# A gated recurrence with routed experts: the last group's loads split into 384 and 64 tokens, and the last block of zeros issued earlier

## Chip, cores and metric

The kernel runs on one core of a Trainium2 chip. The metric is the device time of one execution in microseconds. The kernel before was timed three times; its profile comes from one more execution, taken by the hardware profiler.

## What is computed

First a gated recurrence over 5056 tokens of 4 batches with 256 channels, then a router that gives each of the 20224 tokens to one of 8 experts, of which each keeps the 80 tokens with the largest gate weight. All other rows of the output are zero.

```python
sig = 1.0 / (1.0 + np.exp(-f_logit))
f = lower_bound + (1.0 - lower_bound) * sig          # x, f_logit: (4, 5056, 256)
for t in range(S):
    h = f[:, t] * h + (1.0 - f[:, t]) * x[:, t]
    y[:, t] = h
x = y.reshape(20224, 256)
logits = x @ w_gate                                  # 8 experts
expert_idx = np.argmax(logits, axis=1)
gate_w = softmax(logits)[np.arange(N), expert_idx]
out = np.zeros((N, D))
for e in range(8):
    tok_idx = where(expert_idx == e), the 80 with the largest gate_w
    h = np.maximum(x[tok_idx] @ w1[e], 0.0)          # w1: 256 x 1024
    out[tok_idx] = gate_w[tok_idx, None] * (h @ w2[e])
```

## The kernel before

**Front.** The tokens are taken in 10 groups of 512 (`n_grp`), the last of which (`LAST`, group 9) has 448 in each batch (`TAIL`). A group and a batch make a unit: 40 units, numbered n = 4 x group + batch. A unit loads a tile `f_t` and a tile `x_t` of 128 partitions x 4 tokens x 256 channels, 512 KB each (`load`, L236 and L238). Units of the last group load 512 tokens as well: they start 64 tokens sooner (`tiles`, L156), and `turn_u` and `decay` leave the first 64 out. Then ScalarE takes the sigmoid (`gate`), GpSimd multiplies (`enter`), PE turns both tiles so that channels lie on partitions (`turn_s` into `sp` banks, `turn_u` into `up` banks), ScalarE writes the decay factors into `h_all` (`decay`, L269), DVE runs the recurrence along the tokens (`scan`, L277), and PE makes the router's logits (`logits`). The order is written out by hand: the loop over n from L407 runs `load` four units ahead, `gate` and `enter` two, the turns and `decay` one. Eight buffers (`ring`) hold the loaded tiles, so the load of unit n + 4 waits until PE has turned unit n.

**Ranking.** When the last unit's scan is done, DVE, PE and ScalarE find the 80 kept tokens of each expert; this is one long chain of small steps, mainly on DVE.

**Experts.** For each expert, tokens are copied out of `h_all` one at a time (`gather`), PE multiplies with `w1` (`hidden`) and `w2` (`result`), DVE scales (`finish`, tile `y`), and GpSimd writes 80 rows of the output with an indirect transfer (`scatter`, L783). The weights come as 32 halves of 512 KB (`half`), numbered in the order (1,0), (1,1), (2,0), (1,2), ... of matrix and expert, each matrix in two halves, through seven of the eight buffers: the eighth holds zeros by then. The very last half is loaded in two pieces.

**Zeros.** The output (20.7 MB) is zeroed by transfers that SP issues between the others: `clear` writes zeros from on-chip memory, `copied` (L138) copies the part of the output that is already zero. Some run in the front, many during the ranking, and the last ones between the weights, where the table `BETWEEN` (L529) says behind which half's issue a block stands; the last block has 256 KB. All scatters wait for all blocks of zeros.

All transfers but the scatters are issued by SP, in the order of the program. Each holds one of eight semaphores in turn, and waits until the one that had it before has landed, so SP never has more than eight transfers on their way.

Of the kernel before, what the change touches and what calls it, by code (L numbers as in the profile page):

```python
# [17 lines left out]
P = 128  # L18
# [8 lines left out]
def kernel(  # L27
# [114 lines left out]
    def clear(source):  # L142
# [10 lines left out]
        written[0] += rows * n  # L153

    def tiles(ap, b, g):
        return ap[b, ds(min(first(g), S - G), G)].rearrange("(p r) d -> p r d", r=R)  # L156

# [5 lines left out]
    with tc.tile_pool(name="gsm", bufs=1) as gsm:  # L163
# [69 lines left out]
        def load(n):  # L233
            g, b = divmod(n, B)
            fs[n] = slot(2 * n % NSLOT, "f_t").rearrange("p (r d) -> p r d", r=R)
            nc.sync.dma_start(out=fs[n], in_=tiles(f_logit, b, g))  # L236
            xs[n] = slot((2 * n + 1) % NSLOT, "x_t").rearrange("p (r d) -> p r d", r=R)
            nc.sync.dma_start(out=xs[n], in_=tiles(x, b, g))  # L238

        def gate(n):  # L240
# [7 lines left out]
        def turn_s(n):  # L248
            for o in range(DC):
                ps = pss.tile([P, G], F32, name="sp", tag="sp")  # L250
                for r in range(R):
                    nc.tensor.transpose(ps[:, ds(r * P, P)], sts[n][:, r, ds(o * P, P)], ident)  # L252
                sps[n, o] = ps
            del sts[n]

        def turn_u(n):
            for o in range(DC):
                ps = psu.tile([P, G], F32, name="up", tag="up")
                for r in range(R):
                    nc.tensor.transpose(ps[:, r::R], uts[n][:, r, ds(o * P, P)], ident)  # L260
                ups[n, o] = ps[:, G - size(n // B):]
            del uts[n]
# [3 lines left out]

        def decay(n):
            for o in range(DC):
                nc.scalar.activation(columns(n, o).rearrange("p (k r) -> p k r", r=R),  # L269
                                     sps.pop((n, o)).rearrange("p (r k) -> p k r", r=R)[  # L270
                                         :, P - run(n // B):],
                                     ACT.Identity, scale=nomlb[:, ds(o, 1)], bias=1.0)

        def scan(n):
            for o in range(DC):
                h = columns(n, o)
                nc.vector.tensor_tensor_scan(  # L277
                    h, h, ups.pop((n, o)),
                    h_all[:, o, ds(spot(n - B) + G - 1, 1)] if n >= B else 0.0,
                    ALU.mult, ALU.add)  # L280

        def logits(n):
# [22 lines left out]
        pairs_of.update({g: (g, g + 1) for g in range(LAST - 1, n_grp)})  # L305

        def by_token(g):
            k = run(g)
            ls = lss.pop(g)
            g0 = next(a for a, z in pairs_of.values() if a <= g < z)  # L310
            if g == g0:
                lts[g0] = plt.tile([P, 2, R, P], F32, name="lt", tag="lt")
            for j in range(R):
                nc.tensor.transpose(lts[g0][:k, g - g0, j], ls[:, j::R], ident)  # L314
# [88 lines left out]
        with tc.tile_pool(name="plg", bufs=1, space=PSUM) as plg, \  # L403
             tc.tile_pool(name="plt", bufs=1, space=PSUM) as plt:
            with tc.tile_pool(name="pss", bufs=2, space=PSUM) as pss, \
                 tc.tile_pool(name="psu", bufs=3, space=PSUM) as psu:
                for n in range(-AHEAD, n_unit):  # L407
# [526 lines left out]
```

## Time and profile before

| | us |
|---|---|
| median of three runs | 213.54 (213.47 to 214.17) |
| the profiled execution | 212.61 |
| its span, first to last instruction | 210.8 |
| PE busy | 178.6 (85%) |
| DVE busy | 156.0 (74%) |
| GpSimd busy | 143.2 (68%) |
| ScalarE busy | 133.4 (63%) |
| moved by DMA | 80.60 MB, mean 382 GB/s |

The span is shorter than the execution by what lies before the first and after the last instruction. The busy shares are means over three stages with different limits: the front (to about 126 us), the ranking (to about 152) and the experts. In the rows below PE is TensorE, DVE VectorE, ACT ScalarE, POOL GpSimd, and SPq the queue of SyncE, which issues transfers. "Releaser" is what ended a wait.

### The profile page before, as it was taken

The page shows a single profiled execution, that of the slowest core. Times are in us where ns is not written, and L with a number is a line of the kernel's source. Part 1 is how long each engine was busy: PE and PEld are TensorE (multiplying, and loading weights), DVE is VectorE, ACT ScalarE, POOL GpSimd, SP SyncE. Part 2 cuts the span into 40 slices and gives each one's busy share as a digit, 9 for nine tenths or more (in the row PEclk, how much of TensorE's full clock was granted, in tenths as well). Part 3 has the DMA queues.
Part 4 walks back from the last instruction along what each step waited for, and adds up shares of the span by engine and source line. Part 5 has one row for each costly group of instructions (what it writes and reads, how often), then busy time and mean ns, then how long its engine had stood idle before and what let it go on. Part 6 is the DMA issues. An engine that isn't in the chain of part 4 may idle for free.

```text
span 210.8 us, 6578 instructions
## 1 busy us (share of the span) xinstructions
PE 178.6 (85%) x2091; PEld 140.2 (66%) x2091; DVE 156.0 (74%) x399; ACT 133.4 (63%) x420; POOL 143.2 (68%) x287
## 2 busy tenths in 40 slices
PE   0499989997999999989999886689999697989870
PEld 0498868785878778777878763355586475767540
DVE  5159969999998999899798999975678756461010
ACT  4279789797787778777979872615666555360000
POOL 4848779799797889769897982416666565620372
PEclk9999999999999999999999999797999999999998
DMA  5999999999999999999999999999999999999621
GB/s 214 419 364 398 411 419 448 386 444 394 410 409 414 384 423 375 399 450 386 433 375 408 428 393 371 419 414 432 424 403 404 424 404 420 413 408 410 237 74 51
DMA packets 21362, 80.60 MB, mean 382 GB/s; under 512 B 2580, under 2 KB 2710, under 8 KB 20888
## 3 DMA queue, kind: packets, MB, share of 16 engines
q1 hardware_dynamic: 20936, 79.45, 94.1%
q0 software_dynamic: 384, 0.66, 1.1%
q8 instruction: 18, 0.29, 0.5%
q14 instruction: 24, 0.20, 0.2%
HBM read 72.62 MB, written 21.36 MB: 446 GB/s over the span
## 4 chain that ended last, share of the span: by engine, by line
DMA 34%; PE 33%; ACT 11%; DVE 8%; issue 5%; POOL 4%; ACTq 1%; POOLq 0%; SPq 0%; DVEq 0%
DMA w_sb<-in_moe_w_dram 19%; PE sp L252 11%; PE up L260 9%; DMA x_t<-in_x_dram 8%; PE lg L290 6%; DMA f_t<-in_f_logit_dram 6%; ACT h_all L269 5%; PE lt L314 2%; ACT xe L735 2%; POOL x_t L246 2%; DVE h_all L277 2%; ACT ls L299 2%; PE y_ps L770 2%; POOL out_dram L783 2%; PE h_ps L755 1%
## 5 line engine op out<-in xcount | busy, mean ns | idle before, releaser
L246 POOL TENSOR_TENSOR x_t<-f_t,x_t 128x1024 f32<-128x1024 f32 x40 | 94.8, 2373 | 21.1 <-DMA x_t<-in_x_dram 12.5
L277 DVE TENSOR_TENSOR_SCAN h_all<-h_all,up 128x512 f32<-128x512 f32 (+1 forms) x80 | 95.8, 1245 | 10.4 <-PE up L260 6.5
L269 ACT ACTIVATE h_all<-sp,nomlb 128x512 f32<-128x512 f32 (+1 forms) x80 | 50.3, 678 | 13.6 <-PE sp L252 12.8
L242 ACT ACTIVATE f_t<-f_t 128x1024 f32<-128x1024 f32 x40 | 42.4, 1059 | 11.6 <-DMA f_t<-in_f_logit_dram 9.8
L260 PE MATMUL up<-ident,x_t 128*128 128x128 f32 x320 | 43.8, 279 | 3.1 <-DVE h_all L277 1.8
L252 PE MATMUL sp<-ident,f_t 128*128 128x128 f32 x320 | 45.4, 287 | 0.0
L252 PEld LDWEIGHTS sp<-ident,f_t 128*128 128x128 f32 x320 | 35.9, 145 | 7.7 <-issue 7.3
L260 PEld LDWEIGHTS up<-ident,x_t 128*128 128x128 f32 x320 | 37.0, 144 | 5.0 <-DVE h_all L277 2.9
L735 ACT COPY xe<-h_all 128x2 f32 x256 | 25.4, 191 | 14.6 <-issue 14.1
L735 POOL COPY xe<-h_all 128x2 f32 x192 | 24.4, 187 | 14.6 <-issue 8.3
L770 PE MATMUL y_ps<-w_sb,hid 128*80 128x256 f32 x128 | 29.5, 382 | 4.6 <-DMA w_sb<-in_moe_w_dram 4.6
L735 DVE COPY xe<-h_all 128x2 f32 x192 | 22.6, 176 | 12.2 <-issue 11.0
L770 PEld LDWEIGHTS y_ps<-w_sb,hid 128*80 128x80 f32 x128 | 18.4, 150 | 13.5 <-issue 3.4
L290 PE MATMUL lg<-h_all,wg 128*32 128x128 f32 (+1 forms) x640 | 26.5, 282 | 0.8 <-ACT ls L299 0.6
L755 PEld LDWEIGHTS h_ps<-xe,w_sb 128*64 128x64 f32 x512 | 18.3, 138 | 5.7 <-issue 3.0
L755 PE MATMUL h_ps<-xe,w_sb 128*64 128x80 f32 x512 | 19.5, 234 | 1.0 <-DMA w_sb<-in_moe_w_dram 0.6
L290 PEld LDWEIGHTS lg<-h_all,wg 128*32 128x32 f32 x640 | 15.4, 108 | 7.2 <-issue 4.9
L783 POOL DMA_INDIRECT out_dram<-y,goal x8 | 7.5, 939 | 11.1 <-DMA w_sb<-in_moe_w_dram 9.0
L161 PE MATMUL warm<-h_all,ident 128*128 128x512 f32 x18 | 11.9, 807 | 0.0
L778 DVE TENSOR_SCALAR y<-y_ps,gates 80x256 f32<-80x256 f32 x8 | 3.8, 477 | 10.9 <-PE y_ps L770 10.5
L762 ACT ACTIVATE hid<-h_ps 128x320 f32<-128x320 f32 x8 | 3.5, 435 | 11.3 <-PE h_ps L755 5.8
L314 PE MATMUL lt<-ident,ls 128*128 128x128 f32 (+1 forms) x40 | 7.3, 306 | 3.7 <-ACT ls L299 3.7
(128 smaller groups left out, 98.8 us busy)
## 6 DMA issues: line engine op xcount, KB each, us to landing
f_t<-in_f_logit_dram SPq DMA_DIRECT2D x40, 512.0 KB, 6.4
x_t<-in_x_dram SPq DMA_DIRECT2D x40, 512.0 KB, 6.9
w_sb<-in_moe_w_dram SPq DMA_DIRECT2D x31, 512.0 KB, 9.9
out_dram<-out_dram SPq DMA_DIRECT2D x26, 512.0 KB, 9.8
out_dram<-zbuf SPq DMA_DIRECT2D x12, 512.0 KB, 10.4
out_dram<-h_all SPq DMA_DIRECT2D x1, 512.0 KB, 8.2
w_sb<-in_moe_w_dram SPq DMA_DIRECT2D x2, 256.0 KB, 8.8
out_dram<-out_dram SPq DMA_DIRECT2D x1, 256.0 KB, 9.4
```

Of the source, the lines that this page charges most:

```text
L161: nc.tensor.matmul(warm, ident, h_all[:, 0, :4 * P], start=True, stop=True)
L242: nc.scalar.activation(s_t, s_t, ACT.Sigmoid, scale=-1.0)
L246: nc.gpsimd.tensor_tensor(u_t, sts[n], u_t, ALU.mult)
L252: nc.tensor.transpose(ps[:, ds(r * P, P)], sts[n][:, r, ds(o * P, P)], ident)
L260: nc.tensor.transpose(ps[:, r::R], uts[n][:, r, ds(o * P, P)], ident)
L269: nc.scalar.activation(columns(n, o).rearrange("p (k r) -> p k r", r=R), sps.pop((n, o)).rearrange("p (r k) -> p k r", r=R)[:, P - run(n / ...
L277: nc.vector.tensor_tensor_scan(h, h, ups.pop((n, o)), h_all[:, o, ds(spot(n - B) + G - 1, 1)] if n >= B else 0.0, ALU.mult, ALU.add)
L290: nc.tensor.matmul(lgs[g][ds(q * LC, LC), b, :k].rearrange("p (m i) -> p m i", i=2), wg[:, o], pairs[:, :, q], start=o == 0, stop=o == DC ...
L735: copy(X[e][:, :, ds(k + j, 1)], h_all[:, :, ds(v, 1)])
L755: nc.tensor.matmul(ps[i][ds(s * H, H), c], wo[o][:, at:at + J * (H - 1) + 1:J], xt[:, o], start=o == 0 and c == 0, stop=o == DC - 1, skip_ ...
L770: marks[e, c] = nc.tensor.matmul(y, hid[:, c], halves[c // CH][:, c % CH], start=c == 0, stop=c == FC - 1, skip_group_check=True)
L783: sent.append(nc.gpsimd.indirect_dma_start(out=out, out_offset=bass.IndirectOffsetOnAxis(ap=goal[:, ds(e, 1)], axis=0), in_=rows.pop(e), i ...
```

## The change

The four units of the last group load their first 384 tokens only (three per partition). The other 64 tokens of each batch, in both tensors, come in eight transfers of 64 KB (64 partitions x 256 channels), which go into a part of `h_all` that is not in use yet. Two batches stand below each other, and two such pairs beside each other, so that all of them make one tile of 128 x 2 x 256 for each tensor. They are loaded with units 24 to 31, and get one sigmoid, one product, two times four turns and two decay steps of their own before unit 36 is scanned. The turned products stay in the second half of the `lt` bank, and each scan of the last four units is done in two instructions, 384 and 64 columns. In `BETWEEN` the last entry is 27 for 28.

```diff
     def tiles(ap, b, g):
-        return ap[b, ds(min(first(g), S - G), G)].rearrange("(p r) d -> p r d", r=R)
+        return ap[b, ds(first(g), rows(g) * P)].rearrange("(p r) d -> p r d", r=rows(g))
...
+        rest_f, rest_x = (h_all[:, :, ds(N - i * TAIL, D)] for i in (1, 2))
+
+        def load_rest(i):
+            of, to = ((f_logit, rest_f), (x, rest_x))[i // B]
+            j, c = divmod(i % B, B // DC)
+            nc.sync.dma_start(out=to[ds(c * REST, REST), j], in_=of[i % B, ds(S - REST, REST)])
+
+        def gate_rest():
+            nc.scalar.activation(rest_f, rest_f, ACT.Sigmoid, scale=-1.0)
+
+        def enter_rest():
+            nc.gpsimd.tensor_tensor(rest_x, rest_f, rest_x, ALU.mult)
...
+        def turn_rest(ps, of):
+            for o in range(DC):
+                for j in range(DC):
+                    nc.tensor.transpose(rest_of(ps, o)[:, ds(j * P, P)], of[:, j, ds(o * P, P)],
+                                        ident)
+            return ps
+
+        def decay_rest(sp):
+            for o in range(DC):
+                nc.scalar.activation(
+                    h_all[:, o, ds(LAST * GROUP, B * TAIL)].rearrange(
+                        "p (b t) -> p b t", t=TAIL)[:, :, TAIL - REST:],
+                    rest_of(sp, o).rearrange("p (b t) -> p b t", t=REST),
+                    ACT.Identity, scale=nomlb[:, ds(o, 1)], bias=1.0)
...
                 nc.vector.tensor_tensor_scan(
-                    h, h, ups.pop((n, o)),
+                    h[:, :m], h[:, :m], ups.pop((n, o)),
                     h_all[:, o, ds(spot(n - B) + G - 1, 1)] if n >= B else 0.0,
                     ALU.mult, ALU.add)
+                if g == LAST:
+                    nc.vector.tensor_tensor_scan(
+                        h[:, m:], h[:, m:], rest_of(rest_u, o)[:, ds(b * REST, REST)],
+                        h[:, ds(m - 1, 1)], ALU.mult, ALU.add)
...
+                    if 0 <= m - (TURN - 3 * B) < 2 * B:
+                        load_rest(m - (TURN - 3 * B))
+                    if n == TURN - 4:
+                        gate_rest()
+                    if n == TURN - 3:
+                        enter_rest()
+                    if n == TURN - 2:
+                        decay_rest(turn_rest(pss.tile([P, G], F32, name="sp", tag="sp"), rest_f))
+                    if n == TURN:
+
+                        bank = token_tile(LAST - 1)[:, 1].rearrange("p r k -> p (r k)")
+                        rest_u = turn_rest(bank, rest_x)
                     unit(gate, n + 2)
...
-    BETWEEN = (7, 8, 8, 14, 15, 20, 21, 25, 28)
+    BETWEEN = (7, 8, 8, 14, 15, 20, 21, 25, 27)
```

On SP, in the front (`f_t` and `x_t` are the units' tiles, `out_dram` the zeros), units 24 to 27 stand so before:

```order
L236 DMA f_t<-in_f_logit_dram 128x1024
L238 DMA x_t<-in_x_dram 128x1024
L236 DMA f_t<-in_f_logit_dram 128x1024
L238 DMA x_t<-in_x_dram 128x1024
L236 DMA f_t<-in_f_logit_dram 128x1024
L238 DMA x_t<-in_x_dram 128x1024
L236 DMA f_t<-in_f_logit_dram 128x1024
L238 DMA x_t<-in_x_dram 128x1024
L138 DMA out_dram<-out_dram 16x8192
```

and so the first three of them in the change, where the transfers into `h_all` are the 64 tokens:

```order
L244 DMA f_t<-in_f_logit_dram 128x1024
L246 DMA x_t<-in_x_dram 128x1024
L254 DMA h_all<-in_f_logit_dram 64x256
L244 DMA f_t<-in_f_logit_dram 128x1024
L246 DMA x_t<-in_x_dram 128x1024
L254 DMA h_all<-in_f_logit_dram 64x256
L244 DMA f_t<-in_f_logit_dram 128x1024
L246 DMA x_t<-in_x_dram 128x1024
L254 DMA h_all<-in_f_logit_dram 64x256
```

Behind each of eight units' loads one small transfer has come in; units 28 to 31 have those of `x`.

On SP, near the end of the experts, before (`w_sb` are weight halves, 128x1024 of `w1` and 128x2x512 of `w2`; in brackets what each waits for, DMAHW0 to DMAHW7 being the eight semaphores):

```order
L138 DMA out_dram<-out_dram 16x8192 [waits DMAHW2_49]
L517 DMA w_sb<-in_moe_w_dram 128x1024 [waits DMAHW3_49,PE_49]
L517 DMA w_sb<-in_moe_w_dram 128x1024 [waits DMAHW4_49,PE_49]
L523 DMA w_sb<-in_moe_w_dram 128x2x512 [waits DMAHW5_49,PE_49]
L138 DMA out_dram<-out_dram 16x4096 [waits DMAHW6_49]
L523 DMA w_sb<-in_moe_w_dram 128x2x512 [waits DMAHW7_49,PE_49]
```

and in the change:

```order
L141 DMA out_dram<-out_dram 16x8192 [waits DMAHW2_49]
L581 DMA w_sb<-in_moe_w_dram 128x1024 [waits DMAHW3_49,PE_49]
L581 DMA w_sb<-in_moe_w_dram 128x1024 [waits DMAHW4_49,PE_49]
L141 DMA out_dram<-out_dram 16x4096 [waits DMAHW5_49]
L587 DMA w_sb<-in_moe_w_dram 128x2x512 [waits DMAHW6_49,PE_49]
L587 DMA w_sb<-in_moe_w_dram 128x2x512 [waits DMAHW7_49,PE_49]
```

The last block of zeros (16x4096) and the weight half ahead of it have changed places, and with them their semaphores; the next half keeps its own.

On DVE, at the scans of units 36 and 37, before (`up` holds the turned products):

```order
L277 SCALAR_TENSOR_TENSOR h_all<-h_all,up 128x512 x2
L334 SCALAR_TENSOR_TENSOR eq<-cand,revexp 128x256
L277 SCALAR_TENSOR_TENSOR h_all<-h_all,up 128x448 x4
L343 TENSOR_REDUCE pick<-eq 128x32
L277 SCALAR_TENSOR_TENSOR h_all<-h_all,up 128x448 x2
```

and in the change:

```order
L386 SCALAR_TENSOR_TENSOR eq<-cand,revexp 128x256
L320 SCALAR_TENSOR_TENSOR h_all<-h_all,up 128x384
L325 SCALAR_TENSOR_TENSOR h_all<-h_all,lt 128x64
L320 SCALAR_TENSOR_TENSOR h_all<-h_all,up 128x384
L325 SCALAR_TENSOR_TENSOR h_all<-h_all,lt 128x64
L320 SCALAR_TENSOR_TENSOR h_all<-h_all,up 128x384
L325 SCALAR_TENSOR_TENSOR h_all<-h_all,lt 128x64
L320 SCALAR_TENSOR_TENSOR h_all<-h_all,up 128x384
L325 SCALAR_TENSOR_TENSOR h_all<-h_all,lt 128x64
L395 TENSOR_REDUCE pick<-eq 128x32
```

Each scan has become two, of which the second reads the `lt` bank and starts from the first one's last column.

## Rows read from the trace of the kernel before

**Rows 1.** DMA busy tenths in 40 slices of the span, from the page.

```profile
DMA  5999999999999999999999999999999999999621
```

**Rows 2.** Stretches: length; busy PE, PEld, DVE, ACT, POOL; PE clock, DMA share, GB/s.

```profile
30.00:110.00 80.00, 75.03 (x905) 62.06 (x905) 74.05 (x68) 66.17 (x91) 67.59 (x31) 1.00 1.02 409
110.00:150.00 40.00, 34.10 (x394) 24.05 (x396) 34.58 (x112) 23.71 (x86) 23.45 (x60) 0.91 1.02 410
150.00:198.00 48.00, 43.13 (x570) 31.94 (x566) 26.80 (x185) 24.27 (x220) 23.66 (x169) 1.00 1.01 406
198.00:211.00 13.00, 5.38 (x24) 3.52 (x24) 0.96 (x2) 0.00 (x0) 7.23 (x8) 0.94 0.23 71
```

**Rows 3.** The chain that ended last, shares of the span by line, from the page.

```profile
DMA w_sb<-in_moe_w_dram 19%; PE sp L252 11%; PE up L260 9%; DMA x_t<-in_x_dram 8%; PE lg L290 6%; DMA f_t<-in_f_logit_dram 6%; ACT h_all L269 5%; PE lt L314 2%; ACT xe L735 2%; POOL x_t L246 2%; DVE h_all L277 2%; ACT ls L299 2%; PE y_ps L770 2%; POOL out_dram L783 2%; PE h_ps L755 1%
```

**Rows 4.** Timeline of the tail: start, duration, engine, line, instruction, idle time before.

```profile
196.06 1.93 PE L770 MATMUL y_ps<-w_sb,hid 128*80 128x256 f32 x8
...
197.72 1.13 POOL L783 DMA_INDIRECT out_dram<-y,goal  x1 [8.96 <-DMA w_sb<-in_moe_w_dram]
...
198.75 5.38 PE L770 MATMUL y_ps<-w_sb,hid 128*80 128x256 f32 x24 [0.76 <-DMA w_sb<-in_moe_w_dram]
...
204.17 0.48 DVE L778 TENSOR_SCALAR y<-y_ps,gates 80x256 f32<-80x256 f32 x1 [2.97 <-PE y_ps L770]
...
206.45 0.91 POOL L783 DMA_INDIRECT out_dram<-y,goal  x1 [0.30 <-issue]
```

**Rows 5.** Transfers issued from 186 to 190 us: KB, median us to landing.

```profile
w_sb<-in_moe_w_dram SPq DMA_DIRECT2D x3, 512.0 KB, 9.9
out_dram<-out_dram SPq DMA_DIRECT2D x1, 256.0 KB, 9.4
```

**Rows 6.** Timeline of SP's queue near the end of the experts.

```profile
183.46 1.95 SPq L517 DMA_DIRECT2D w_sb<-in_moe_w_dram  x2
186.80 0.38 SPq L523 DMA_DIRECT2D w_sb<-in_moe_w_dram  x1
187.26 0.52 SPq L138 DMA_DIRECT2D out_dram<-out_dram  x1
188.74 3.86 SPq L523 DMA_DIRECT2D w_sb<-in_moe_w_dram  x4
```

**Rows 7.** DMA queues from 196 to 211 us: packets, MB, share of 16 engines.

```profile
q0 software_dynamic: 384, 0.66, 14.9%
```

**Rows 8.** DMA from 30 to 110 us, then from 3 to 8 us.

```profile
DMA packets 8173, 32.71 MB, mean 409 GB/s; under 512 B 996, under 2 KB 996, under 8 KB 8050
...
DMA packets 559, 2.00 MB, mean 401 GB/s; under 512 B 68, under 2 KB 70, under 8 KB 559
...
h_all<-in_moe_w_gate_dram SPq DMA_DIRECT2D x1, 8.0 KB
h_all<-in_lower_bound_dram SPq DMA_DIRECT2D x1, 1.0 KB
```

**Rows 9.** SP's queue around the first expert, and transfers issued from 146 to 147 us.

```profile
146.53 0.52 SPq L138 DMA_DIRECT2D out_dram<-out_dram  x1
149.41 0.35 SPq L517 DMA_DIRECT2D w_sb<-in_moe_w_dram  x1
...
150.73 0.38 SPq L523 DMA_DIRECT2D w_sb<-in_moe_w_dram  x1
...
out_dram<-out_dram SPq DMA_DIRECT2D x1, 512.0 KB, 10.9
```

**Rows 10.** Groups by shape from 100 to 130 us: count, busy us, mean ns.

```profile
L246 POOL TENSOR_TENSOR x_t<-f_t,x_t 128x1024 f32<-128x1024 f32 x8 | 19.1, 2381 | 3.0 <-DMA x_t<-in_x_dram 1.6 <-PE sp L252 1.0
L277 DVE TENSOR_TENSOR_SCAN h_all<-h_all,up 128x512 f32<-128x512 f32 x11 | 13.5, 1266 | 2.0 <-PE up L260 1.9
...
L277 DVE TENSOR_TENSOR_SCAN h_all<-h_all,up 128x448 f32<-128x448 f32 x8 | 8.6, 1124 | 0.0
```

**Rows 11.** Issues of the whole span: KB each, median us to landing, from the page.

```profile
f_t<-in_f_logit_dram SPq DMA_DIRECT2D x40, 512.0 KB, 6.4
```

More of the change, by code (lines that the diff above doesn't have):

```diff
@@ L69 @@
     assert TAIL % C == 0 and (GROUP & (GROUP - 1)) == 0
+    REST = TAIL % P
+    assert REST * B == DC * P and TAIL > P
     SEG = N // C
@@ L153, in clear, with rows @@
         written[0] += rows * n
+    def rows(g):
+        return size(g) // P
     def tiles(ap, b, g):
-        return ap[b, ds(min(first(g), S - G), G)].rearrange("(p r) d -> p r d", r=R)
+        return ap[b, ds(first(g), rows(g) * P)].rearrange("(p r) d -> p r d", r=rows(g))
     def busy(pool, m, tag):
@@ L234, in load, with rest_of @@
             g, b = divmod(n, B)
-            fs[n] = slot(2 * n % NSLOT, "f_t").rearrange("p (r d) -> p r d", r=R)
+            k = rows(g)
+            fs[n] = slot(2 * n % NSLOT, "f_t").rearrange("p (r d) -> p r d", r=R)[:, :k]
             nc.sync.dma_start(out=fs[n], in_=tiles(f_logit, b, g))
-            xs[n] = slot((2 * n + 1) % NSLOT, "x_t").rearrange("p (r d) -> p r d", r=R)
+            xs[n] = slot((2 * n + 1) % NSLOT, "x_t").rearrange("p (r d) -> p r d", r=R)[:, :k]
             nc.sync.dma_start(out=xs[n], in_=tiles(x, b, g))
+        rest_f, rest_x = (h_all[:, :, ds(N - i * TAIL, D)] for i in (1, 2))
[7 more added lines that the diff above has]
+            nc.gpsimd.tensor_tensor(rest_x, rest_f, rest_x, ALU.mult)
+        def rest_of(ap, o):
+            return ap[:, ds(o * B * REST, B * REST)]
+        def turn_rest(ps, of):
[11 more added lines that the diff above has]
+                    ACT.Identity, scale=nomlb[:, ds(o, 1)], bias=1.0)
         def gate(n):
@@ L250, in turn_s @@
                 ps = pss.tile([P, G], F32, name="sp", tag="sp")
-                for r in range(R):
+                for r in range(rows(n // B)):
                     nc.tensor.transpose(ps[:, ds(r * P, P)], sts[n][:, r, ds(o * P, P)], ident)
@@ L258, in turn_u @@
                 ps = psu.tile([P, G], F32, name="up", tag="up")
-                for r in range(R):
-                    nc.tensor.transpose(ps[:, r::R], uts[n][:, r, ds(o * P, P)], ident)
-                ups[n, o] = ps[:, G - size(n // B):]
+                k = rows(n // B)
+                for r in range(k):
+                    nc.tensor.transpose(ps[:, r:k * P:k], uts[n][:, r, ds(o * P, P)], ident)
+                ups[n, o] = ps[:, :k * P]
             del uts[n]
@@ L267, in decay @@
         def decay(n):
+            r = rows(n // B)
             for o in range(DC):
-                nc.scalar.activation(columns(n, o).rearrange("p (k r) -> p k r", r=R),
-                                     sps.pop((n, o)).rearrange("p (r k) -> p k r", r=R)[
-                                         :, P - run(n // B):],
+                nc.scalar.activation(columns(n, o)[:, :r * P].rearrange("p (k r) -> p k r", r=r),
+                                     sps.pop((n, o))[:, :r * P].rearrange("p (r k) -> p k r", r=r),
                                      ACT.Identity, scale=nomlb[:, ds(o, 1)], bias=1.0)
         def scan(n):
+            g, b = divmod(n, B)
+            m = rows(g) * P
             for o in range(DC):
@@ L305, with token_tile @@
         pairs_of.update({g: (g, g + 1) for g in range(LAST - 1, n_grp)})
+        def token_tile(g0):
+            if g0 not in lts:
+                lts[g0] = plt.tile([P, 2, R, P], F32, name="lt", tag="lt")
+            return lts[g0]
         def by_token(g):
@@ L311, in by_token @@
             if g == g0:
-                lts[g0] = plt.tile([P, 2, R, P], F32, name="lt", tag="lt")
+                token_tile(g0)
             for j in range(R):
```

## The prediction

> **What bounds the kernel now.** I read the line of DMA busy shares first: 9 in every slice from the second to the 37th [rows 1]. The table by stretch says the same with numbers: share 1.02, 1.02 and 1.01 at 409, 410 and 406 GB/s from 30 to 198 us, then 0.23 [rows 2]. No engine is as full: in the first stretch PE has 75.0 of 80 us, DVE 74.1, and in the expert stretch no one but PE is above 27 of 48. The chain of waits agrees: its largest line is the weight transfers [rows 3]. So up to 198 us the time is bytes over a rate, and after it there is a tail of 12.6 us in which hardly anything is moved.
>
> The tail has two strands [rows 4]. One is weights: the last transfer that PE waits for lands at 198.62 (issued at 188.74, 9.88 us later), PE does 24 multiplications from 198.75, and the last scaling of `y` stands at 204.17 + 0.48 = 204.65. The other is the scatters. All eight stand behind the last zero block; the first starts on GpSimd at 197.72 after 8.96 us of idling, they follow each other, and the eighth starts at 206.45, 1.80 after its `y` was ready. So the scatters end last, and their start is set by the zeros. (The row names a weight transfer as the releaser, and the zero block had landed at 187.26 + 9.4 = 196.66 [rows 5]; the first scatter's wait in the program is for the transfers that wrote zeros. A rival below takes the label at its word.)
>
> **The change part by part.** All is counted on the profiled execution: 212.61 us, of which 210.8 are the span and 1.8 lie around it. The median of the runs is 213.54, 0.93 more; I take a gain over from the one to the other unchanged.
>
> *The last zero block.* SP keeps eight transfers in flight: each waits for the one eight before it. That is why the block was issued at 187.26 and the weight half ahead of it at 186.80 [rows 6]. In the change these two swap their turns. The queues are served in order, so the block's bytes stand 512 KB sooner: 524,288 B / 406 GB/s = 1.29 us. Bounds: if only the issue counted, 187.26 - 186.80 = 0.46. If it could go right behind the half before it (the row at 183.46 ends at 185.41), 1.85; but the last `y` at 204.65 plus the 0.30 of idling that stands before a scatter caps the gain at 206.45 - 204.95 = 1.50. I take 1.29, nearest to a queue in order. The weight half that steps back lands 0.63 later (256 KB); PE took it up at 196.06, spent 1.93 on its eight multiplications and then waited 0.76 for the next half anyway, whose place does not move. That wait covers it; without it, it would cost 0.63 on the strand of `y`, which has 1.80 to give.
>
> *The bytes removed.* Units 36 to 39 load 384 tokens for 512, two tensors each: 8 x 128 rows lose 1 KB, 1,048,576 B / 409 GB/s = 2.56 us.
>
> *The bytes added.* Eight transfers of 64 rows of 1 KB: 524,288 B, by bytes 1.28 us. No load of such rows stands in the trace. The nearest rows from above are the scatters: 640 rows of 1 KB take 14.9% of 16 engines x 15 us = 35.8 us of engine time, 56 ns a row [rows 7], so 512 x 56 / 16 = 1.79 us. For a price per transfer there is the start of the program: 3 to 8 us holds the two smallest transfers of all, 8 KB and 1 KB, and still has 401 GB/s against the 409 of a stretch without any [rows 8]; 8/409 of 5 us is 0.10, 0.05 for each, which makes 1.28 + 8 x 0.05 = 1.68. The net saving is 2.56 - 1.28 = 1.28 at best, 0.77 by the scatters, 0.88 by the start. I take 0.9. The other end, far off, is a small transfer as dear as a 512 KB one, 1.28 each: 10.25 - 2.56 = 7.7 lost.
>
> A row can speak against this only for the placement: each of these transfers fills 64 partitions, and every large one of before fills 128. The Trainium skill (SBUF — State Buffer, "Door 1: The DMA port swizzle") says that partitions 0 to 63 reach only half of the DMA ports of the memory. By that rule the added bytes would take 2.56 us and the net saving would be 0; no run here shows it. It is the first rival.
>
> *Where the saving goes.* The loads are in the front; it reaches the end only if the queues never run dry between. The place to look is where SP waits for PE: the copy issued at 146.53 is the last before the first expert's weights free a buffer at 149.41 [rows 9]. That copy lands 10.9 later, at 157.4, so some 8 us of work were queued, and with 0.9 less it is 7 us. From 149.41 on SP issues again (three in 1.32 us), faster than they drain. So 0.9 arrives at every later landing, the last one at 198.62 included, and both strands of the tail move by it.
>
> *The engines in the front.* Cost in the sum: none, because of those 7 us. What they do all the same: DVE has 1266 ns for 512 columns and 1124 for 448 [rows 10], 2.2 ns a column and 138 fixed; so 384 + 64 columns cost 983 + 279 = 1262 for 1124, eight times, +1.1 us, on the stretch that leads to the ranking. GpSimd's product costs 2381 ns on 1024 elements; ¾ of that four times saves 2.4, and the product of the 64-token part adds half of one, 1.2, some units sooner. PE loses 16 transposes and gains 8. ScalarE gains three instructions, sigmoid and decay of the rest, and has shorter ones in the last four units. SP gains eight issues of about 0.33; it idles there. The rest waits for its loads nowhere, since they are issued 8 or more units ahead of their use. Even if all of it came late, DVE's 1.1 and one GpSimd product of 1.2, the ranking would slip by 2.3, and there are 7.
>
> *What is queued behind new waits.* On PE the four transposes of the rest need a free `sp` bank and those into the `lt` bank need the DVE step that read it; behind them stand the unit's own transposes, which free the load buffers. A stall of 1 to 2 us there takes from the 6.4 us that a load is on its way [rows 11] and leaves the queues full.
>
> **Sum:** 1.29 + 0.9 = 2.2 us. Span 208.6, execution 210.4, median 213.5 - 2.2 = **211.3**. The likeliest case's own range joins 0.46 to 1.50 with 0.77 to 1.28, so gains of 1.2 to 2.8: 210.7 to 212.3.
>
> **Rivals.**
> 1. The rest's rows land at half the rate, so the bytes give nothing: only the zeros' 1.29 is left, 212.2. For it: half the partitions. Against it: part of what is in flight at the time, a quarter to a third of the transfers, doesn't go by the same half, and the eight alternate between halves.
> 2. The first scatter waits for something else than the zeros, as its row says [rows 4]: 196.66 to 197.72 are 1.06 us without an explanation. Then the swap gives nothing and only 0.9 remains: 212.6. Against it: the half that PE took up at 196.06 had landed by then, the next at 198.62, so no weight landing that a row shows fits 197.6.
> 3. Slower: each small transfer holds the queues for a fixed piece of time, beyond its bytes. Place: the front, units 24 to 31. It decides from (2.56 + 1.29) / 8 = 0.48 us for each; at 1.28 for each, like a 512 KB load, the execution is 10.25 - 2.56 - 1.29 = 6.4 longer, 219.9. For it: eight more transfers among only eight in flight. Against it: the two tiny ones at the start [rows 8]. The Trainium skill speaks for it (DMA: Bandwidth & Descriptors, "Measured"): a 64 KB transfer spans 0.95 us there. As an estimate from that page, 8 x 0.95 - 3.85 = 3.8 longer, 217.3; the trace of the start disagrees with such a price in a full queue.
> 4. The change doesn't do what it says: the scatters wait as before, and the saved bytes are lost in a gap of the queues. 213.5.
>
> **How the numbers follow.** Forecast 0.60, rival 1 0.14, rival 2 0.10, rival 4 0.06, rival 3 0.10. A measurement here can tell about 0.3%, 0.64 us, from no change, so faster means below 212.9. Forecast and rival 1 are there, rival 2 in two thirds of its cases: 0.80. Within 0.3%: rival 4 and the rest of rival 2, 0.10. Slower: rival 3, 0.10. The range 210.5 to 213.2 holds the forecast with its bounds and rivals 1 and 2, and leaves out rivals 3 and 4 and some tails, 0.2.
>
> **What would show it.** Moved bytes 80.60 - 0.52 = 80.1 MB. The last zero block is issued ahead of the weight half and the first scatter starts near 195.5, the eighth near 204.3; PE's last wait for weights ends near 197.8. Right for the bytes: the last large load and all later landings come about 0.9 sooner, with a DMA share of 1.0 on both sides of 149. Wrong: a first scatter that moves no more than the weights (rival 2); a front whose last load lands no sooner (rival 1) or later (rival 3); a dip of the DMA share between 140 and 155, which would say that the ranking became the bound; or an eighth scatter that starts right behind its `y`, which would say that the cap was reached.

## The result: slower

The changed kernel takes 216.32 us (median of 4 runs, 214.54 to 217.98) against 213.5 of the kernel before in the same job: a ratio of 1.0139, 95% interval 1.0091 to 1.0187, that is 3.0 us (1.9 to 4.0) more. The forecast was 211.3, with a range of 210.5 to 213.2. The profile is that of its longest run, 217.98 with a span of 215.9, which counts as a slow run and is left out of the ratio; the run e2_rest below, which differs only in the place of the last zeros, was profiled in a fast run at 216.6 and shows the same three places (367 GB/s from 84 to 100 us, a share of 0.89 from 113 to 120 and of 0.95 from 156 to 168).

The DMA line and the four stretches, from the page and the table by stretch of the changed kernel (columns as in [rows 2]):

```profile
DMA  6999999999999999999997999999989999999621
```

```profile
30.00:110.00 80.00, 73.37 (x883) 60.13 (x886) 70.63 (x66) 63.69 (x89) 64.69 (x30) 1.00 1.02 402
110.00:150.00 40.00, 30.45 (x349) 23.27 (x339) 34.61 (x90) 21.77 (x52) 21.59 (x35) 0.93 0.98 384
150.00:198.00 48.00, 45.17 (x559) 32.12 (x559) 29.62 (x214) 27.71 (x259) 27.34 (x195) 0.95 1.01 392
198.00:211.00 13.00, 10.87 (x103) 7.68 (x101) 1.93 (x4) 0.44 (x1) 6.69 (x8) 1.00 0.53 194
```

Against [rows 1, 2]: the 9s have two gaps, and the rate is lower in all three full stretches (402, 384 and 392 GB/s for 409, 410 and 406). What was not moved there is moved after 198 us, at 194 GB/s for 71. Shorter stretches show where, first before, then after:

```profile
84.00:100.00 16.00, 14.24 (x170) 11.73 (x170) 14.94 (x16) 12.28 (x18) 12.69 (x7) 1.00 1.00 408
113.00:120.00 7.00, 6.38 (x86) 5.15 (x86) 7.00 (x6) 5.94 (x9) 6.71 (x4) 1.00 1.09 447
150.00:156.00 6.00, 5.67 (x86) 3.94 (x83) 4.66 (x39) 4.22 (x41) 4.50 (x35) 1.00 1.05 425
156.00:168.00 12.00, 9.62 (x113) 6.87 (x113) 8.51 (x61) 8.29 (x80) 7.98 (x58) 1.00 1.00 400
```

```profile
84.00:100.00 16.00, 13.28 (x151) 10.64 (x148) 13.11 (x15) 11.29 (x16) 11.95 (x7) 1.00 1.00 364
113.00:120.00 7.00, 6.51 (x86) 5.18 (x87) 5.16 (x7) 5.13 (x9) 5.14 (x3) 1.00 0.89 319
150.00:156.00 6.00, 6.00 (x38) 3.12 (x39) 4.06 (x36) 4.15 (x45) 4.07 (x31) 0.63 1.05 419
156.00:168.00 12.00, 12.00 (x197) 9.20 (x194) 8.01 (x61) 8.54 (x82) 8.76 (x65) 1.00 0.93 328
```

Read share and rate together. From 84 to 100, where the last of the small transfers run (they are issued from 69.6 to 93.5), the share is 1.00 in both kernels and the rate falls from 408 to 364: the DMA engines are as busy and move less. From 113 to 120 and from 156 to 168 the share falls as well (1.09 to 0.89, 1.00 to 0.93): for part of the time they have nothing to do. So there are three places. SP's issues of `f_t` name what feeds the first two; here are those of units 32 and 39, before and after:

```profile
91.35 0.33 SPq L236 DMA_DIRECT2D f_t<-in_f_logit_dram  x1
...
112.30 0.33 SPq L236 DMA_DIRECT2D f_t<-in_f_logit_dram  x1
```

```profile
94.07 0.52 SPq L244 DMA_DIRECT2D f_t<-in_f_logit_dram  x1
...
116.42 0.33 SPq L244 DMA_DIRECT2D f_t<-in_f_logit_dram  x1
```

Unit 32 is 2.7 late behind the small transfers, unit 39 4.1. The weights stand behind unit 39 in SP's queue, so nothing fills the gap from 113 on. The third place is that of [rows 9]:

```profile
149.05 0.52 SPq L141 DMA_DIRECT2D out_dram<-out_dram  x1
156.59 0.35 SPq L581 DMA_DIRECT2D w_sb<-in_moe_w_dram  x1
```

SP waits 7.5 us between two issues where it waited 2.9. What it waits for is the first expert, whose matrix products free a weight buffer. Two starts on PE mark the way there: that of the products that write `kept`, the list of the kept tokens, near the end of the ranking (called "kept" from here on), and that of the first expert's (`h_ps`, "expert 0"). Before, then after:

```profile
140.16 1.02 PE L687 MATMUL kept<-put,what 128*8 128x80 bf16 x24
...
148.04 2.44 PE L755 MATMUL h_ps<-xe,w_sb 128*64 128x80 f32 x64
```

```profile
145.90 1.02 PE L751 MATMUL kept<-put,what 128*8 128x80 bf16 x24
...
155.21 2.44 PE L819 MATMUL h_ps<-xe,w_sb 128*64 128x80 f32 x64
```

Kept is 5.7 late and expert 0 is 7.2. The other 1.4 are PE's clock: between the two starts PE does the same 92 instructions without a pause, but its granted clock (the number ahead of the DMA share) is 0.63 where it was 0.79, first before, then after:

```profile
140.20:148.00 7.80, 7.80 (x92) 4.69 (x91) 4.21 (x35) 3.34 (x33) 3.50 (x25) 0.79 1.04 425
```

```profile
145.90:155.20 9.30, 9.30 (x92) 6.36 (x91) 5.43 (x44) 4.06 (x41) 4.23 (x31) 0.63 1.04 420
```

The tail, against [rows 4]:

```profile
202.17 1.13 POOL L847 DMA_INDIRECT out_dram<-y,goal  x1 [8.53 <-DMA w_sb<-in_moe_w_dram]
202.36 7.11 PE L834 MATMUL y_ps<-w_sb,hid 128*80 128x256 f32 x32 [0.59 <-DVE hid L827]
...
209.50 0.48 DVE L842 TENSOR_SCALAR y<-y_ps,gates 80x256 f32<-80x256 f32 x1 [2.97 <-PE y_ps L834]
...
210.92 0.91 POOL L847 DMA_INDIRECT out_dram<-y,goal  x1 [0.30 <-issue]
```

It has the same shape, 4.4 to 5.3 us later.

### The profile page after: what moved, and what is told of

It is laid out like the page before. It is cut to its first block, busy times and chain, and to the rows that moved or that the text cites. A ratio compares the mean times of both kernels' runs of the same rounds, so it can differ in the third digit from the quotient of the medians.

```text
span 215.9 us, 6593 instructions
## 1 busy us (share of the span) xinstructions
PE 180.3 (84%) x2083; PEld 141.4 (65%) x2083; DVE 156.9 (73%) x407; ACT 132.8 (61%) x423; POOL 142.5 (66%) x288
## 4 chain that ended last, share of the span: by engine, by line
PE 45%; DMA 29%; DVE 11%; ACT 6%; issue 3%; POOL 3%; SPq 0%; DVEq 0%; POOLq 0%; ACTq 0%
DMA w_sb<-in_moe_w_dram 12%; PE sp L292 11%; PE up L301 9%; PE y_ps L834 8%; DMA f_t<-in_f_logit_dram 7%; PE lg L337 6%; DMA x_t<-in_x_dram 6%; DMA out_dram<-out_dram 4%; DVE h_all L320 4%; ACT h_all L311 3%; PE warm L168 3%; PE h_ps L819 3%; PE lt L366 2%; POOL x_t L286 2%; PE slots L751 2%
## 5 line engine op out<-in xcount | busy, mean ns | idle before, releaser
L286 POOL TENSOR_TENSOR x_t<-f_t,x_t 128x1024 f32<-128x1024 f32 (+1 forms) x40 | 92.6, 2317 | 24.8 <-DMA x_t<-in_x_dram 11.2
L282 ACT ACTIVATE f_t<-f_t 128x1024 f32<-128x1024 f32 (+1 forms) x40 | 41.5, 1038 | 14.7 <-DMA f_t<-in_f_logit_dram 13.2
L301 PEld LDWEIGHTS up<-ident,x_t 128*128 128x128 f32 x312 | 36.3, 145 | 7.1 <-POOL x_t L286 4.1
L799 DVE COPY xe<-h_all 128x2 f32 x192 | 22.7, 176 | 11.8 <-issue 10.5
L366 PEld LDWEIGHTS lt<-ident,ls 128*128 128x128 f32 (+1 forms) x40 | 5.5, 207 | 8.6 <-ACT ls L346 7.1
L168 PE MATMUL warm<-h_all,ident 128*128 128x512 f32 x18 | 10.5, 718 | 0.0
```

Source lines behind the costliest of these rows:

```text
L168: nc.tensor.matmul(warm, ident, h_all[:, 0, :4 * P], start=True, stop=True)
L282: nc.scalar.activation(s_t, s_t, ACT.Sigmoid, scale=-1.0)
L286: nc.gpsimd.tensor_tensor(u_t, sts[n], u_t, ALU.mult)
L301: nc.tensor.transpose(ps[:, r:k * P:k], uts[n][:, r, ds(o * P, P)], ident)
L799: copy(X[e][:, :, ds(k + j, 1)], h_all[:, :, ds(v, 1)])
```

## The experiments

All were timed beside the kernel before; "cost" is the ratio to it (with its 95% interval) in microseconds. The columns of times are read from the one profile of each: the issue of unit 39's `f_t`, the starts of kept and of expert 0, and the span. The cost is over all runs and the times are of one, so they need not agree to the microsecond.

| kernel | ratio (95%) | cost, us | unit 39 | kept | expert 0 | span |
|---|---|---|---|---|---|---|
| before | 1 | 0 | 112.30 | 140.16 | 148.04 | 210.8 |
| changed | 1.0139 (1.0091 to 1.0187) | +3.0 | 116.42 | 145.90 | 155.21 | 215.9 |
| e1_zeros | 0.9990 (0.9959 to 1.0020) | -0.2 | 112.72 | 140.44 | 148.37 | 211.1 |
| e2_rest | 1.0199 (1.0157 to 1.0241) | +4.2 | 115.16 | 144.92 | 154.25 | 214.6 |
| e3_small | 1.0129 (1.0093 to 1.0165) | +2.7 | 114.84 | 142.61 | 151.99 | 213.7 |
| e4_none | 1.0025 (0.9991 to 1.0060) | +0.5 | 114.19 | 143.76 | 151.69 | 212.0 |
| e6_112 | 1.0166 (1.0119 to 1.0212) | +3.5 | 112.20 | 143.14 | 152.24 | 214.9 |
| e7_half | 1.0005 (0.9972 to 1.0038) | +0.1 | 112.15 | 139.97 | 150.47 | 211.2 |
| e8_two | 0.9983 (0.9962 to 1.0003) | -0.4 | 113.32 | 141.08 | 149.01 | 211.1 |
| e9_scans | 1.0159 (1.0108 to 1.0210) | +3.4 | 112.33 | 145.27 | 153.06 | 213.6 |
| e10_copies | 1.0022 (0.9986 to 1.0058) | +0.5 | 113.49 | 141.21 | 149.04 | 211.4 |
| e11_less | 0.9993 (0.9960 to 1.0026) | -0.1 | 111.99 | 139.02 | 146.95 | 209.7 |
| e12_wide | 1.0084 (1.0046 to 1.0122) | +1.8 | 113.84 | 143.41 | 151.34 | 212.3 |
| e13_onescan | 1.0089 (1.0060 to 1.0118) | +1.9 | 115.05 | 141.97 | 151.30 | 213.3 |
| e14_four | 1.0029 (0.9995 to 1.0063) | +0.6 | 112.74 | 143.70 | 151.63 | 212.5 |
| e15_inline | 0.9976 (0.9936 to 1.0016) | -0.5 | 111.97 | 140.03 | 147.91 | 211.0 |

From kept to expert 0 it is 7.8 to 7.9 us in most of the profiles, but 9.1 to 9.4 in the changed kernel, e2, e3, e6 and e13 and 10.5 in e7, each time at a lower granted clock. No run varies the clock, so how much of their costs is due to it stays open.

### The two parts apart: e1_zeros and e2_rest

```diff
 # e1: before, with the zeros' move alone
-    BETWEEN = (7, 8, 8, 14, 15, 20, 21, 25, 28)
+    BETWEEN = (7, 8, 8, 14, 15, 20, 21, 25, 27)
 # e2: the changed kernel, with the last entry back at 28
```

> The kernel before with one entry of BETWEEN changed, 28 to 27: only the last block of zeros changes its turn. Theory A (the zeros' step of the prediction was right, and what made the change slower is the rest): the first scatter starts 0.5 to 1.5 us sooner, the eighth too, and the time is 212.0 to 213.0 us, some 1.3 below the kernel before. Rival (the zeros' step itself does harm, since the weight half behind it lands later and PE then ends last): 213.5 or above.

> The changed kernel with the last entry of BETWEEN back at 28: only the loads and the work of the 64 tokens are left of the change. Theory A (all the loss comes from these, and at the end of the changed kernel PE's last results decide and not the scatters' start): 215.5 to 217.5 us, like the changed kernel. Rival (the zeros' turn does the harm): 212 to 213.5.

The zeros' move gains nothing that can be told from none, at most 0.9 us, and the loss is the loads': with the zeros back in their old place it is there still (e2). Between e2 and the changed kernel the intervals overlap, so what the move is worth there stays open. The tail of e1:

```profile
196.84 1.13 POOL L783 DMA_INDIRECT out_dram<-y,goal  x1 [7.87 <-DMA w_sb<-in_moe_w_dram]
...
197.10 7.20 PE L770 MATMUL y_ps<-w_sb,hid 128*80 128x256 f32 x32 [0.67 <-DVE hid L763]
...
204.34 0.48 DVE L778 TENSOR_SCALAR y<-y_ps,gates 80x256 f32<-80x256 f32 x1 [2.97 <-PE y_ps L770]
...
205.57 0.92 POOL L783 DMA_INDIRECT out_dram<-y,goal  x1 [0.30 <-issue]
```

Against [rows 4] the first and the eighth scatter start 0.88 sooner, so the zeros did set them. But PE does its 32 multiplications in one piece from 197.10 and ends them at 204.30, no sooner than before, and the last `y` stands at 204.82 for 204.65. From the eighth scatter's start to the end of the span it is 5.5 us, for 4.35 before. That stretch is 4.3 to 6.0 us over the sixteen profiles, whatever the kernel, so one profile of each can't say whether the 0.88 reaches the end, and the interval of the cost (0.9 gained to 0.4 lost) ends about there.

### What the small transfers cost: e3_small, e4_none, e7_half, e8_two

```diff
 # e3: before, with the change's eight transfers, which nothing reads
+    nc.sync.dma_start(out=to[ds(c * 64, 64), j], in_=of[i % B, ds(S - 64, 64)])
 # e7: the same 64 KB each, over 128 partitions
+    nc.sync.dma_start(out=to[:, j, ds(c * P, P)],
+                      in_=of[i % B, ds(S - 64, 64)].rearrange("t (h d) -> (t h) d", d=P))
 # e8: the same 0.52 MB in two transfers, 128 partitions x 2 KB
+    nc.sync.dma_start(out=to, in_=of[0, ds(0, 2 * P)].rearrange("(p j) d -> p j d", j=DC))
 # e4: the changed kernel without the transfers
-    load_rest(m - (TURN - 3 * B))
+    nc.gpsimd.memset(rest_f, 0.0)       # and rest_x, once
```

> The kernel before with the eight 64 KB transfers issued behind the loads of units 24 to 31 and used by nobody; last units load 512 tokens as before. So 0.52 MB more are moved, 1.28 us at 409 GB/s. Theory A1 (the small transfers are dear in the front: the changed kernel's load of unit 32 was issued 2.7 us later): the load of unit 32 is issued 2.7 us later than before, and the time is about 216.2 us. Theory A2 (they cost their bytes, and the work on the 64 tokens made the rest of the delay): load of unit 32 about 1.3 us later, 214.8 us.

> The changed kernel without the eight small transfers: two memsets on GpSimd fill their place, so the results for the last 64 tokens of each batch are left out; all other work on them stays. 2.56 us of bytes fewer than before. Theory A1 (small transfers dear): loads of unit 32 are issued as before, unit 39 about 1.4 us later than before (turns of the rest on PE), the ranking slips by 2.5 to 3.5 us and the queues do not run dry, 210 to 211.5 us. Theory A2 (the work on the 64 tokens makes the slip): the last scan still ends 4 us or more later than before, a dip of the DMA share after 150 us, 213 to 215.5 us.

> The kernel before with eight added 64 KB transfers that nothing uses, as in the run with eight of 64 partitions x 1 KB, but spread over 128 partitions, in rows of 512 bytes. If it is the 64 partitions that made those dear (2.75 us for 1.28 us of bytes), these cost 1.3 us: 214.2. If it is each transfer (0.34 us), the cost stays at 2.75: 215.6. If it is each row (86 ns of one engine's time a row, 1024 rows on 16 engines), it doubles to 5.5: 218.4.

> The kernel before with the same 0.52 MB added in two transfers of 256 KB, 128 partitions x 2 KB, that nothing uses. If each transfer costs 0.34 us, two cost 0.7 us at least, and the bytes 1.28: 214.2. If each row costs 86 ns whatever its length, 256 rows cost 1.4 us: 214.3. If cost goes by bytes at 409 GB/s, 1.28: 214.2. A cost near 2.75 (215.6) would say that any added transfer of these sizes is dear, or that the delay, not the bytes, counts.

The stretch of the small transfers, in e3, then in e7:

```profile
84.00:100.00 16.00, 13.20 (x147) 10.28 (x145) 13.43 (x15) 11.53 (x17) 12.15 (x7) 1.00 1.01 373
```

```profile
84.00:100.00 16.00, 14.20 (x168) 11.49 (x167) 14.54 (x15) 11.81 (x17) 12.23 (x6) 1.00 1.03 414
```

Eight transfers of 64 KB cost 2.7 us (2.0 to 3.5) on 64 partitions and 0.1 (-0.6 to 0.8) on 128, with twice as many rows of half the length. So neither the count of transfers nor that of rows makes the cost, only the partitions: on 64 the engines are as busy (1.01) at 373 GB/s, on 128 they move 414. It is seen in the front already: unit 32's load goes out 2.7 late in e3 and 0.4 late in e7. The rule of rival 1 (the Trainium skill, "SBUF — State Buffer", "Door 1: The DMA port swizzle") puts the eight on 64 partitions, as an estimate, at 2.56 us; the run agrees in size. That the eight alternate between the halves did not help. What no theory had (they gave 214.2 at least): over all partitions the 0.52 MB, 1.28 us by bytes, cost 0.8 at most, in eight transfers or in two. 408 GB/s at a share of 1.00 was no limit. (In e8's one profile unit 39 and expert 0 are 1.0 late, so in the front itself the bytes are not always free; such a delay is hidden later, as e14 below shows.)

e4 leaves the transfers out and gains nothing (0.5 behind, -0.2 to 1.3), though it moves 2.56 us fewer bytes than before. Its kept is 3.6 us late, and the queue runs dry from 113 to 120 (share 0.91, 315 GB/s).

### What the removed bytes are worth: e11_less and e10_copies

```diff
 # e11: the last units load 3 of 4 tokens a partition and turn the third twice
-    nc.sync.dma_start(out=fs[n], in_=tiles(f_logit, b, g))
+    nc.sync.dma_start(out=fs[n], in_=tiles(f_logit, b, g)[:, :size(g) // P])
 # e10: two of the copies of zeros moved into the front
-    elif 3 < m < TURN and m % 4 == 3:
+    elif 3 < m < TURN and (m % 4 == 3 or m in (17, 25)):
```

> The kernel before, whose last eight units load 384 of their 512 tokens (1.05 MB less, 2.56 us at 408 GB/s) and take the third quarter for the fourth as well: the results of those tokens are left out, no instruction is added, VectorE's scans stay as they were. It measures what the removed bytes are worth by themselves. Theory V (VectorE paces the front): the loads are issued when slots come free, as before (u39 at 112.3), the saved time shows as a queue that runs dry between 100 and 120, and the time is 212.3 to 212.9. Theory B (bytes count): 210.2. By the prediction on record it would be 1.05 MB less with nothing added: 2.56 us, less what the front cannot use.

> The kernel before with two more of the 512 KB copies of zeros issued in the front (ahead of the loads of units 18 and 26), so that two fewer are left between the weights; the bytes in all are the same. Theory V (the front is paced by VectorE, and transfers over all 128 partitions cost nothing there, as the two runs with 0.52 MB more showed at 212.83 and 212.55; behind 113 us the DMA engines set the pace): the two copies are free where they go and leave 2 x 1.28 = 2.56 us where they were: 210.2, or 211.5 if one of them is. Rival S (a copy in the front delays the loads behind it on SP by its 1.28 us, as the gaps of 3.77 instead of 2.5 us between loads behind each copy would say): the ranking starts 2.56 us later and the end is 212.8 to 215.4.

The full 2.56 us of bytes with nothing added brought 0.1 us, at most 0.85: theory V. Unit 39's load goes out at 111.99 for 112.30, because it waits for a buffer, not for the engines. SP's waits in the kernel before say so for the whole front: of its 40 loads of `f_t`, 34 waited for PE's turns to free a buffer (total us, times, longest), and so did 34 of `x_t`:

```profile
SPq L236 <- PE sp L252: 50.6, 34, 3.9
SPq L238 <- PE up L260: 18.2, 34, 1.4
```

From 113 to 120 e11 moves less for it:

```profile
113.00:120.00 7.00, 7.00 (x95) 6.04 (x84) 7.00 (x8) 5.79 (x10) 5.16 (x3) 1.00 1.00 344
```

344 GB/s for 447: what was saved went unused. The mean share is still 1.00, but the busy tenths from 113 to 117 us show the gaps, first before, then in e11:

```profile
DMA  9999899999998999997999899999999989989969
```

```profile
DMA  4749789998799669723976967698999081232999
```

Moving zeros into the front (e10) did not pay either: in its profile two copies delay unit 39 by 1.2 us. That is neither the 2.56 of rival S nor the 0 of theory V, so by this profile the front has some room, but less than for 1 MB.

### What a late ranking costs: e9_scans and e14_four

```diff
+    if n // B == LAST:                       # e14: and n % B < 2
+        nc.vector.tensor_tensor_scan(more, h[:, :64], h[:, 64:128], 0.0, ALU.mult, ALU.add)
```

> The kernel before with eight added scans of 64 columns on VectorE, one behind each scan of the last units, whose result nothing uses; not a byte more is moved. Theory E (VectorE's row of work in the front is on the path): 8 x 0.27 to 0.35 = 2.2 to 2.8 us later at the last scan, the kept matmuls as much later (142.4 to 143.0 instead of 140.2), and the end 1.5 to 2.8 us later: 214.4 to 215.7. Rival M (some 7 us of transfers are queued ahead at 149 us and hide it): the kept matmuls as much later, the end within 0.3%: 212.9. Rival D (VectorE has gaps that take them up): the kept matmuls at 140.2 to 140.8, the end at 212.9.

> The kernel before with four added scans of 64 columns instead of eight, behind the scans of units 36 and 37, whose result nothing uses. Theory R (a reserve: in the profile of eight added scans the first expert's start moved by 5.0 us and the span by 2.8, so some 2.2 us are hidden and all beyond is paid): the kept matmuls start 1.1 to 2.5 us later than before, at 141.3 to 142.7, and the end stays within 0.3 to 0.5 us of before, 212.8 to 213.3. Rival C (every delay of the ranking is paid at the same share): half of what eight cost, 214.5.

Eight added scans, not a byte more: 3.4 us (2.3 to 4.5). Four: 0.6 (-0.1 to 1.3). The delays were larger than expected (kept 5.1 and 3.5 late for 2.8 and 2.5 at most), because two of the scans took about 1.3 us instead of 0.29 in both kernels. The scans are not those of the change, which took 0.35 in all eight places; the pair measures what a delay costs. 3.5 us of delay cost little, the next 1.6 cost 2.8 (1.0 at the least, by the intervals). That is theory R: a reserve hides the first part. In e9 SP issues nothing from 146.79 to 154.44, and the stretches show when the queue is empty:

```profile
150.00:153.00 3.00, 3.00 (x6) 1.03 (x4) 1.47 (x13) 2.01 (x22) 2.08 (x15) 0.72 1.13 466
153.00:156.00 3.00, 3.00 (x67) 2.61 (x67) 2.57 (x23) 2.17 (x23) 2.03 (x16) 1.00 0.66 214
```

Full until 153, running dry after it: the queued work keeps all engines busy for 6.2 us, of which before needs 2.9 (149.41 - 146.53 in [rows 9]), which leaves a reserve of 3.3 us. By the spans it is smaller: expert 0 is 5.0 and 3.6 late in e9 and e14, the spans are 2.8 and 1.7 longer, so 2.2 and 1.9 are hidden. So the reserve is 2 to 3.3 us. e7 agrees: its first expert starts 2.4 late, since PE had a granted clock of 0.52 from 140 to 150, near the lower of its two levels (1.2 and 2.4 GHz), after it had been busy for 5.0 of the 10 us before; and that costs nothing.

### The change without its costs: e12_wide, e13_onescan, e15_inline

```diff
 # e12: the changed kernel, each transfer over 128 partitions
-    nc.sync.dma_start(out=to[ds(c * REST, REST), j], in_=of[i % B, ds(S - REST, REST)])
+    nc.sync.dma_start(out=to[:, j, ds(c * P, P)], in_=...rearrange("t (h d) -> (t h) d", d=P))
 # e13: and the products turned in the unit's own bank, one scan of 448
+    nc.tensor.matmul(ps[:, ds(k * P, REST)], rest_u[j][:, ds(c * P, P)], ident[:, o::DC], ...)
-                if g == LAST:                # the second scan
 # e15: and `f` likewise, with a decay step a unit; decay_rest is gone
+    nc.tensor.matmul(ps[:, ds(k * P, REST)], rest_f[:, j, ds(c * P, P)], ident[:, o::DC], ...)
```

> The changed kernel, with its eight 64 KB transfers spread over 128 partitions in rows of 512 bytes (each half of a row on a partition of its own), and the last block of zeros where the kernel before has it or one half sooner as in the change. Two causes (64 partitions cost 2.75 us of loads; added scans and turns cost 3.6 us of ranking, of which the saved bytes give most back): the loads of units 32 and 39 are issued at 91.6 and 114.2, the kept matmuls start at 143.8, as in the run without these transfers, and the time is that run's, 213.6 (213.0 to 214.2). If any transfer of 64 KB was dear: 216.3, as the changed kernel.

> The run with wide transfers, and in addition the rest's 64 columns turned by one short matmul a unit and half straight behind the unit's own 384 columns, so that one scan of 448 takes both: no scans are added to VectorE, and no turn of the rest waits for the bank of the logits. Theory V (VectorE's added work made the ranking late): the last scan and the kept matmuls come 2.2 us sooner than in the run with wide transfers, at 141.2 to 141.8, and the time is 212.5 to 213.2. If the slip came from the turns and the decay of the rest instead, the kept matmuls stay at 143 or later and the time at 213.6.

> The run with wide transfers and single scans, and in addition the rest's part of `f` turned by one short matmul a unit and half into the unit's own bank, with a decay step of its own for the 64 columns: nothing of the rest is done in one lump any more. Theory L (the lump put off the last loads, and the weights stand behind them in SP's queue): the wait of 1.7 us for `h_all` ahead of unit 35's scans goes, the load of unit 39 is issued at 112.0 to 113.0 instead of 115.05, the kept matmuls start at 140 to 141, and the time is that of before, 212.5 to 213.2. Theory B (once its costs are gone the change gains by its 0.52 MB): 211.5. If neither is so and it stays at 214.3, something else in the change costs the time.

All three keep the change's place of the last zeros. Wide transfers take 1.2 us off (3.0 to 1.8; by the two intervals, taken as independent, -0.1 to 2.5), and unit 32 goes out 0.4 late for 2.7: the cause is there, but the expected 213.6 was missed by 1.4. Single scans take nothing off; that expectation failed. In e13's profile kept comes 1.4 sooner than in e12's, but expert 0 does not (151.30 for 151.34), since the granted clock between them was 0.63 for 0.78; so what the scans cost stays open. What is left in both is the lump: four turns and two decay steps of the rest at one place, behind which DVE waits ahead of unit 35's scans, in e13:

```profile
115.62 2.45 DVE L326 TENSOR_TENSOR_SCAN h_all<-h_all,up 128x512 f32<-128x512 f32 x2 [1.73 <-ACT h_all L319]
```

All five kernels with the lump (changed, e2, e4, e12, e13) have this wait, 1.7 to 1.8 us. Unit 39's load is late by 1.5 in e12 and 2.75 in e13, and the weights behind it; 0.4 and 1.6 of that are there at unit 32, ahead of the lump, so the lump adds 1.2 in both, and 1.1 to 1.6 over the five. In e12, then in e15:

```profile
113.00:120.00 7.00, 6.88 (x89) 5.54 (x90) 5.43 (x6) 6.15 (x11) 5.53 (x3) 1.00 0.80 281
```

```profile
113.00:120.00 7.00, 7.00 (x99) 6.23 (x88) 6.88 (x7) 5.86 (x13) 4.97 (x4) 1.00 0.99 355
```

With the turns and decay steps spread over the units (e15) the wait is gone, unit 39 goes out at 111.97, the share is 0.99 for 0.80, and 2.4 us come back (by the intervals 1.4 to 3.4): theory L. Against e12, which has the same 7.9 us from kept to expert 0, it is 2.3, so by the profiles this is not the clock. The result, 0.9976 (0.9936 to 1.0016), cannot be told from before: once its costs are gone, the change lies between 0.3 us lost and 1.4 gained.

### Another way to load 448 tokens: e6_112

```diff
-        return ap[b, ds(min(first(g), S - G), G)].rearrange("(p r) d -> p r d", r=R)
+        return ap[b, ds(first(g), size(g))].rearrange("(p r) d -> p r d", r=R)   # 112 partitions
```

> The kernel before, whose last units load exactly their 448 tokens, as 112 partitions of four tokens: 0.52 MB less is moved, with no second transfer and no second scan (the scans stay at 1.09 us each, 448 columns). Theory B (bytes alone decide): the last load is issued 1.28 us sooner and the time falls by as much, to 211.6 (ratio 0.994). Theory E (VectorE's scans in the front are the second bound, 2.2 us a unit against 2.5 us of load): the loads come 1.3 us sooner, the ranking at most 0.5 us sooner, and the rest shows as an emptier queue between 113 and 120 or near 150: 212.4 to 213.2. Theory H (fewer than 128 partitions land more slowly): the eight transfers take as long as before, u39 is issued at 112.3 as before, and the time is 212.9.

None of the three: unit 39's load goes out as theory H says, but the cost is 3.5 us. From 113 to 120 the engines are full and move 262 GB/s, and from 100 to 113 the transfers of 448 KB need 9.0 us to land where the one of 512 KB needs 5.4:

```profile
100.00:113.00 13.00, 12.48 (x152) 10.62 (x154) 11.84 (x12) 10.62 (x15) 9.40 (x5) 1.00 1.01 336
113.00:120.00 7.00, 5.52 (x81) 4.21 (x80) 5.23 (x6) 4.21 (x7) 4.70 (x3) 1.00 1.04 262
```

```profile
f_t<-in_f_logit_dram SPq DMA_DIRECT2D x4, 448.0 KB, 9.0
...
f_t<-in_f_logit_dram SPq DMA_DIRECT2D x1, 512.0 KB, 5.4
```

## Why the prediction was wrong

- **"Up to 198 us the time is bytes over a rate."** This is where it failed first. A share of 1.0 was taken as a limit; in the front it is not one. There the units follow DVE and PE, a load waits for its buffer (34 of 40), and 0.52 MB more (e7, e8) or 1.05 MB less (e11) change nothing that can be measured. The 2.56 us for the removed bytes are 0.1, at most 0.85. The rows had signs of it: DVE with 74.05 of 80 us [rows 2], and a chain in which PE's turns and logits (`sp`, `up`, `lg`) have 26% and the loads 14% [rows 3]; the prediction read only its largest line.
- **The bytes added, 1.68 us.** Measured 2.7 (2.0 to 3.5, e3), outside the bounds taken (1.28 to 1.79). Rival 1 is right that the 64 partitions are dear, and its price (2.56) fits; its time was not, because it gave the zeros a gain and the engines no cost. Rival 3, the one on the slower side, had the sign right by luck: on 128 partitions eight transfers cost 0.1 (e7), so it is not a price for each transfer.
- **"A stall of 1 to 2 us there … leaves the queues full."** The stall came as described, 1.8 us, and the queues ran dry in part from 113 to 120. The 6.4 us that a load is on its way did not cover it, because the weights cannot be issued ahead of the last load. The sum had this at nothing; the lump costs 2.4 us (e13 to e15).
- **"The ranking would slip by 2.3, and there are 7."** Both numbers were off. Kept slipped by 3.6 without the small transfers (e4) and by 5.7 with them, expert 0 by 7.2, and the reserve is 2 to 3.3 us, not 7. The 10.9 us to landing in [rows 9] is when the last transfer ends; the sixteen engines together are full for 6.2 (e9). The dip that the prediction named as the sign of this came later than it looked for it, from 156 to 168.
- **DVE's 1.1 us.** The pieces of 384 and 64 columns cost about what was worked out (pairs 1.30 apart for 1.09, 1.7 over eight). That this adds to the end by itself is not shown: e13 removes it and gains nothing, but at a lower clock in its profile.
- **The zeros, 1.29 us.** The scatters did start 0.88 sooner in e1, inside the bounds, so rivals 2 and 4 are wrong on this mechanism. The time did not clearly follow: 0.2, at most 0.9. The prediction let both strands of the tail move, but the strand of `y` had only the bytes' gain, which did not come.

So the loss comes from the 64 partitions and the lump, through two gaps: late last loads with the weights behind them (113 to 120), and a first expert later than the reserve (156 to 168). Taken out one after the other they give back 1.2 and 2.4 us, which is the whole loss within its interval. The first costs 2.7 alone and 1.2 here; they may overlap, but the intervals do not show it, and neither how much each adds in the changed kernel nor what PE's lower clock adds there was separated further.

## What to carry to other kernels

A full DMA share says that the engines hold work, not that bytes bound the time: look whether the next transfer is issued when one lands or when an engine frees its buffer, and price bytes only in the first case. Transfers of a split-off remainder were dear on 64 partitions and cost next to nothing on 128 here, so spread them, and put the remainder's work into the steps of the units it came from, not into one lump ahead of the last load. How long a queue covers a wait is read from where the share falls, or the span grows, when the wait grows, not from the time to landing of its last transfer.

## What the runs showed of the hardware

- Eight transfers of 64 KB on 64 partitions made the kernel 2.7 us longer (e3), about what twice their bytes would take at 409 GB/s (2.56); the same bytes on 128 partitions, in rows of 512 bytes, 0.1 (e7).
- Loads of 112 partitions are far worse than 112/128: 262 GB/s at a share of 1.04 (e6, 113 to 120), where loads of 128 partitions had 408 at 1.00 (before, 84 to 100). The cause was not looked for.
- An added scan of 64 columns, both inputs from `h_all`, took 0.29 us in five places of eight, 0.45 in one and 1.28 and 1.30 in two (e9). Those two ran while GpSimd was at its products of 2.4 us (114.98 to 122.23), as did the two long scans (1.28 and 1.29) of e14; the change's scans of 64 columns, with one input from the `lt` bank, took 0.35 beside such products too. No run varies this alone.
